# Pinning TensorE's issue order, splitting the load of p, and two w_out tiles with buffers of their own

## The chip, the core and the metric

The kernel runs on one core of a Trainium2 chip. The metric is the device time of one launch in microseconds (us). TensorE (PE) multiplies, VectorE (DVE), ScalarE (ACT) and GpSimd (POOL) work element by element, and SyncE (SP) issues nearly all DMAs. Each engine works through its own stream of instructions in the order in which they were issued to it, and waits on semaphores for the others.

## What is computed

```python
def sm_attn(qq, kk, vv):                      # softmax(qq kk^T / 8) vv
    ...
p_packed = sm_attn(p, k, v)                   # 32 rows per head
x = sm_attn(q, p_packed, p_packed)            # (4, 8, 576, 64) -> (2304, 512)
h = x @ w_in                                  # (2304, 2048)
x = (max(h, 0) + log1p(exp(-abs(h)))) @ w_out # (2304, 512)
out = (sigmoid(x @ w_gate) * (x @ w_val)) @ w_out2
```

q, k, v and p come in float32; the weights come in float64 and are turned into float32 on DVE from their two 32-bit words.

## The kernel before

**Attention** runs in 8 units (batch b, head group g of four heads). A unit is a generator of 11 stages (`attn_unit`, line 330): three stages of transposes of k (L333 is the transpose of p, L313 those of k and q), then the first scores (L326, with kT and pT) and their softmax on DVE and ACT (L345 to L357, up to the DVE transpose a1T), three stages of transposes of q, the product with v (L369), the second scores (L326, with qT and ppT), and the second softmax (L391 to L409), whose result is split into a high part A2h (ACT, L410) and a low part A2l (POOL, L101 with A2l). `att_tick` advances one live unit by one stage; up to four units run ahead before the first layer.

**The first layer** goes over entries (b, c), b a batch and c one of 8 chunks of 256 columns of w_in. The matrix p_packed is first multiplied into w_in (`prep_wp`, L480, then ACT writes the high part wph at L487, DVE or POOL the low part wpl at L101). `emit_h` then does 12 matmuls into one h tile (L113, L114, L115: the high and low products of A2 and wp), followed by softplus on ACT (L509 to L511) and DVE (L519, tile g). `emit_out1` multiplies the result ghl with w_out two entries later (L537, L538, L540) and DVE adds it into xa (L98 or L545). In the program's text `emit_h` of an entry stands ahead of the `emit_out1` of an older entry and ahead of the attention stages called between its pieces.

**The second layer** (L812 to L867, from about 400 us) is untouched but for two helpers through which its matmuls now go.

**What sets the order.** The text fixes one order in which instructions are traced. The framework then plans each engine's stream itself with a model of times: an instruction whose inputs it takes to be ready may be issued ahead of one that stands before it in the text. SP's stream is planned in the same way, and its DMAs wait there for the buffers that they write.

**Loads.** `load_kqv` (line 229) gives k, q, v tiles of 576 KB to ten places: eight in xa and NEXT = 2 tiles `own0`, `own1`; a tile is loaded when a place comes free. `load_next` (line 144) loads the next weight tile from the list `order` (two tiles of w_in chunk 0, two of w_out chunk 0, two of w_in chunk 1, and so on) into one of two `raw` buffers; `convert` (L189, L194, L198 on DVE) frees it and calls `load_next` again. p, 0.5 MB, is loaded by two DMAs on ACT's queue (L275) into `pall`, for all 8 units at once.

Of the kernel before, what the change touches and what calls it, by code (L numbers as in the profile page):

```python
# [11 lines left out]
I32 = mybir.dt.int32  # L12
# [8 lines left out]
def attn_moe_moe_kernel(  # L21
# [24 lines left out]
    nc = tc.nc  # L46
    B, H, S, D = q.shape
    NK = p.shape[2]
    NT, DM = out.shape
    F1 = w_in.shape[1]  # L50
    F2 = w_gate.shape[1]
    P = 128
# [6 lines left out]
    KD = DM // P  # L59
# [8 lines left out]
    L0 = 3  # L68
    GP = 7
    PO = ['k0', 'q0', 'k1', 'v0', 'q1', 'v1']  # L70
    XR = 0
    EARLY = [0]
    NCV = 5
    SC = float(D) ** -0.5
# [11 lines left out]
    xa = cst.tile([P, KD * NT], F32, name="xa")  # L86
# [16 lines left out]
    def pool_hi(hi, x):  # L103
        nc.gpsimd.tensor_scalar(hi, x, 1.0, 0.0, op0=ALU.mult, op1=ALU.add)

    def hi_of(on_act, hi, x):
        if on_act:
            nc.scalar.activation(hi, x, AF.Copy)  # L108
        else:
            pool_hi(hi, x)  # L110

    def mm3(ps, wh, wl, xh, xl, first, last):
        nc.tensor.matmul(ps, wh, xh, start=first, stop=False)  # L113
        nc.tensor.matmul(ps, wh, xl, start=False, stop=False)  # L114
        nc.tensor.matmul(ps, wl, xh, start=False, stop=last)  # L115

    nc.scalar.preload_act_table_set("natural_log_exp_and_others")

    att = tc.alloc_tile_pool(name="att", bufs=1, side="right")
# [14 lines left out]
    for c in range(NCH1):  # L134
        order += [("in", c, f) for f in range(2)] + [("out", c, f) for f in range(2)]
        if c > ECS:
            n = -(-len(early) // (NCH1 - c))
# [6 lines left out]
    def load_next():  # L144
        if not waiting:
            return
        nm, c, f = key = waiting.popleft()
        if XR and key == ("out", 0, 0):

            t = xa[:, : 2 * DM].bitcast(I32).rearrange("p (n t) -> p n t", t=2)  # L150
        else:
            t = raw.tile([P, KD * P, 2], I32, tag="raw", name="raw_" + nm)
        a = c * CF + f * P
        if nm in ("out", "o2"):
            nc.sync.dma_start(t.rearrange("p n t -> p (n t)"), w32[nm][a : a + P, :])
        elif nm == "in":

            for g in range(2):
                nc.sync.dma_start(
                    t[64 * g : 64 * g + 64].rearrange("p (k n) t -> p k (n t)", k=KD),  # L160
                    w32[nm][256 * g : 256 * g + 256, 2 * a : 2 * (a + P)].rearrange(
                        "(k p) x -> p k x", p=64
                    ),
                )
        else:
            nc.sync.dma_start(
                t.rearrange("p (k n) t -> p k (n t)", k=KD),
                w32[nm][:, 2 * a : 2 * (a + P)].rearrange("(k p) x -> p k x", p=P),
            )
        raws[key] = t  # L170
# [41 lines left out]


    KQV = 2 * NC * D
    NEXT = 2
    own = [att.tile([P, KQV], F32, name=f"own{i}") for i in range(NEXT)]
    plan = deque((nm, u) for u in range(2 * B) for nm in "kqv")
    first = sorted((plan.popleft() for _ in range(6)), key=lambda x: PO.index(x[0] + str(x[1])))
# [3 lines left out]
    def place(u):  # L222

        for tag in [*range(2 * (u // 2), 2 * B), *range(2 * B, 2 * B + NEXT)]:
            if tag not in busy:
# [37 lines left out]
    ident = cst.tile([P, P], F32, name="ident")  # L263
# [7 lines left out]


    pall = att.tile([P, 2 * B, 2, D], F32, name="pall")
    for i in range(2):
        nc.scalar.dma_start(  # L275
            pall[:, :, i], p.rearrange("b (g h) n d -> (h n) (b g) d", g=2)
        )

    NWORK = 7
    SPL = []  # L280
# [27 lines left out]
    def turned(src, dst):  # L308

        for i in range(0, NC, 3):  # L310
            ps = bank1()
            for c in range(i, i + 3):
                nc.tensor.transpose(  # L313
                    ps[:, (c - i) * P : (c - i + 1) * P], src[:, c * P : (c + 1) * P], ident
                )
            o = dst[:, i : i + 3].rearrange("p c n -> p (c n)")
            nc.scalar.activation(o, ps[:, : 3 * P], AF.Copy)
            yield

    def scores(lhsT, xT, to):  # L320

        for e in range(2):
            r = slice(64 * e, 64 * e + 64)
            for h in range(4):
                n = slice(NK * h, NK * h + NK)
                nc.tensor.matmul(  # L326
                    to[e][n], lhsT(r, h), xT[r, :, n], start=True, stop=True
                )

    def attn_unit(u):  # L330
        b, g = divmod(u, 2)
        px = bank1()
        nc.tensor.transpose(px[:, :P], pall[:, u].rearrange("p i d -> p (i d)"), ident)  # L333
        pT = att.tile([P, P], F32, tag="pT", bufs=2, name="pT")
        nc.scalar.activation(pT, px[:, :P], AF.Copy)
        kT = att.tile([P, NC, P], F32, tag="kT", bufs=1, name="kT")
# [28 lines left out]
        for e in range(2):  # L365
            for c in range(NC):
                for h in range(4):
                    r = slice(NR * h, NR * h + NR)
                    nc.tensor.matmul(  # L369
                        pp[h // 2][64 * (h % 2) : 64 * (h % 2) + 64, :NK],  # L370
                        vt[r, c, e, :], a1T[r, e * NC + c, :],
                        start=e == c == 0, stop=(e, c) == (1, NC - 1),
                    )
# [75 lines left out]
    w_in_f, wo_hl, Wp = {}, {}, {}  # L449
# [18 lines left out]
    def prep_wp(items):  # L468

        n = len(items)  # L470
        hi, lo = (
            ph1.tile([P, 2, 2, CF], F32R, tag="wp" + y, bufs=NWP, name="wp" + y)[:, :n]
            for y in "hl"
        )
        ps = [bank1().rearrange("p (i n) -> p i n", i=2)[:, :n] for _ in range(2)]
        for i, (b, c) in enumerate(items):
            for h in range(4):
                for t in range(2):
                    r = slice(64 * t, 64 * t + 64)
                    nc.tensor.matmul(  # L480
                        ps[t][NK * h : NK * h + NK, i], ppT[r, b, 4 * t + h, :],
                        w_in_f[c][r, h, :], start=True, stop=True,
                    )
            Wp[b, c] = (hi[:, i], lo[:, i])
        for t in range(2):
            if n == 1 or items[0][0] == items[1][0]:
                nc.scalar.activation(hi[:, :, t], ps[t], AF.Copy)  # L487
                split_lo(nc.vector, lo[:, :, t], ps[t], hi[:, :, t])
            else:
                x = new_cv().rearrange("p (i n) -> p i n", i=2)  # L490
                nc.scalar.activation(x, ps[t], AF.Copy)
                pool_hi(hi[:, :, t], x)
                split_lo(nc.gpsimd, lo[:, :, t], x, hi[:, :, t])
            yield
# [33 lines left out]
    def emit_out1(b, c, s, att_ticks):  # L528
        finish(f"wo{c}")
        gh, gl = gt.pop((b, c, s))  # L530
        for m in range(KD):
            ms = slice(m * P, (m + 1) * P)
            ps = bank1()
            out_ = ps[:, :HS]
            for f in range(2):
                wh, wl = wo_hl[c, f]
                nc.tensor.matmul(out_, wh[:, ms], gh[:, f], start=f == 0, stop=False)  # L537
                nc.tensor.matmul(out_, wl[:, ms], gh[:, f], start=False, stop=False)  # L538
            for f in range(2):
                nc.tensor.matmul(out_, wo_hl[c, f][0][:, ms], gl[:, f], start=False, stop=f == 1)  # L540
            dst = x2(b, s)[:, m]
            if c == 0:
                copy(CP0, dst, out_)
            else:
                nc.vector.tensor_tensor(dst, dst, out_, op=ALU.add)  # L545
            between(m, att_ticks)
# [147 lines left out]
    load_kqv(6)  # L694
    for _ in range(2):
        load_next()
    units.extend(range(2 * B))
    n = 0
    jobs.append(("win0", prep_win(0)))
# [18 lines left out]
    for i, (b, c) in enumerate(entries):  # L718
# [9 lines left out]
        if c >= 2 and b % 2 == 0:  # L728
# [3 lines left out]
            if k + 1 < len(groups):  # L732
                x, cc = groups[k + 1]
# [33 lines left out]
            pend.append((b, c, s))  # L767


    if PRE:  # L770
        tc.keep_in_program_order(nc.scalar.preload_act_table_set("sigmoid_and_others"))
    while pend:
        emit_out1(*pend.popleft(), [0] * 3)
# [79 lines left out]
    def emit_out2(ps, c, t):  # L853
        bank = bank1()
        ts_ = slice(t * P, (t + 1) * P)
        for f in range(2):
            gh, gl = (y.rearrange("p b s t -> p (b s t)") for y in gv[ps, 2 * c + f])
            _, _, oh, ol = Bop[ps, 2 * c + f]
            nc.tensor.matmul(bank, gh[:, ts_], oh, start=f == 0, stop=False)  # L859
            nc.tensor.matmul(bank, gh[:, ts_], ol, start=False, stop=False)  # L860
            nc.tensor.matmul(bank, gl[:, ts_], oh, start=False, stop=f == 1)  # L861
        i = KD * HS * HB * 2 * ps + DM * t
        acc = xa[:, i : i + DM]
        if c == 0:
            copy(CPA, acc, bank)
        else:
            nc.vector.tensor_tensor(acc, acc, bank, op=ALU.add)  # L867
        tick()
        if c == NCH2 - 1:
            t0 = ps * HB * S + t * P  # L870
            a, e = t0, t0 + P
            while a < e:
                b, r = divmod(a, S)
                ee, cc = divmod(r // NR, NC)
                nc.sync.dma_start(outv[b, ee, cc], acc[a - t0 : a - t0 + NR])
                a += NR
# [63 lines left out]
```

## Time and profile before

| | us |
|---|---|
| median of 3 runs | 885.74 (882.08 to 887.05) |
| the profiled execution | 884.71 |
| its span | 882.9 |
| outside the span | 1.8 |
| PE busy | 823.5 (93%) |
| DVE, POOL, ACT busy | 626.0, 451.9, 376.3 |

PE is the busiest engine by far, so its idle time and the stretches in which its clock was granted at half are what can be won back. A row of the timeline has start, duration, engine, line, operation, tiles and count, and in brackets the engine's idle time before it with what ended it.

### The profile page before, as it was taken

The numbers are of one execution on the slowest core, as the hardware profiler recorded it, in microseconds if no ns is written. First come the engines' busy times: TensorE is split into PE (matmuls) and PEld (weight loads), VectorE is DVE, ScalarE is ACT, GpSimd is POOL, SyncE is SP. The second block draws the span as 40 slices with busy tenths as digits, with TensorE's granted clock in tenths as the row PEclk, the third lists the DMA queues.
The fourth block names the chain that finished last, engine by engine and source line by source line (L and its number), as shares of the span: only waits on it lengthen the run. The fifth ranks groups of instructions, "written<-read, shape, count | busy, mean of one in ns | idle before, by whom it ended". The sixth has DMA issues, their size and how long they took to land.

```text
span 882.9 us, 17370 instructions
## 1 busy us (share of the span) xinstructions
PE 823.5 (93%) x7040; PEld 755.4 (86%) x7040; DVE 626.0 (71%) x1057; ACT 376.3 (43%) x659; POOL 451.9 (51%) x420
## 2 busy tenths in 40 slices
PE   2976999999999999998999999999989999999995
PEld 1655788889989999998989999999869999999984
DVE  0757676778686577558898688897898656766763
ACT  1453666466555556666633331232342432322210
POOL 0043232366473555576469687886883633634400
PEclk9787999999999999998999999999999999999998
DMA  8644030123152223100055454645435312213004
GB/s 266 220 139 122 28 110 29 31 67 97 39 172 60 49 70 110 43 25 1 1 170 177 155 168 150 186 129 157 139 87 141 86 48 71 79 44 95 13 1 107
DMA packets 52480, 85.67 MB, mean 97 GB/s; under 512 B 6960, under 2 KB 30640, under 8 KB 52400
## 3 DMA queue, kind: packets, MB, share of 16 engines
q1 hardware_dynamic: 50320, 84.04, 32.5%
q8 instruction: 55, 0.90, 0.4%
q10 hardware_dynamic: 2080, 0.52, 0.3%
q14 instruction: 25, 0.20, 0.1%
HBM read 65.67 MB, written 18.87 MB: 96 GB/s over the span
## 4 chain that ended last, share of the span: by engine, by line
PE 77%; DVE 11%; ACT 3%; DMA 3%; issue 3%; POOL 2%; SPq 0%; POOLq 0%; ACTq 0%; DVEq 0%
PE bank L115 9%; PE bank L113 9%; PE bank L114 9%; PE ps L537 6%; PE ps L540 6%; PE ps L538 6%; PE ps L861 5%; PE ps L859 5%; PE ps L860 5%; PE ps L115 3%; PE ps L114 3%; PE ps L113 3%; DMA pall<-in_p_dram 2%; PE ps L369 2%; PE ps L313 2%
## 5 line engine op out<-in xcount | busy, mean ns | idle before, releaser
L113 PE MATMUL bank<-aop,BH 128*128 128x288 f32 x672 | 198.8, 296 | 3.7 <-DVE work L824 1.5
L114 PE MATMUL bank<-aop,BH 128*128 128x288 f32 x672 | 197.9, 295 | 1.0 <-DVE aop L101 0.9
L115 PE MATMUL bank<-aop,BL 128*128 128x288 f32 x672 | 198.6, 296 | 0.0
L101 POOL TENSOR_TENSOR ghl<-g,ghl 128x576 fp32r<-128x576 f32 x64 | 93.8, 1469 | 133.5 <-ACT ghl L108 133.5
L537 PE MATMUL ps<-ghl,woh 128*128 128x288 f32 x512 | 148.7, 305 | 6.0 <-DVE xa L545 3.6
L538 PE MATMUL ps<-ghl,wol 128*128 128x288 f32 x512 | 144.6, 297 | 0.0
L545 DVE TENSOR_TENSOR xa<-xa,ps 128x288 f32<-128x288 f32 x224 | 97.2, 448 | 59.0 <-PE ps L540 58.0
L113 PEld LDWEIGHTS bank<-aop,BH 128*128 128x128 f32 x672 | 126.2, 188 | 9.1 <-issue 1.4
L114 PEld LDWEIGHTS bank<-aop,BH 128*128 128x128 f32 x672 | 126.4, 188 | 5.1 <-DVE aop L101 1.6
L115 PEld LDWEIGHTS bank<-aop,BL 128*128 128x128 f32 x672 | 126.5, 188 | 0.0
L101 POOL TENSOR_TENSOR BL<-cv,BH 128x512 fp32r<-128x512 f32 (+1 forms) x96 | 116.8, 1231 | 11.3 <-ACT BH L108 10.2
L537 PEld LDWEIGHTS ps<-ghl,woh 128*128 128x128 f32 x512 | 97.4, 190 | 15.9 <-DVE xa L545 6.2
L540 PE MATMUL ps<-ghl,woh 128*128 128x288 f32 x512 | 110.6, 297 | 0.1
L538 PEld LDWEIGHTS ps<-ghl,wol 128*128 128x128 f32 x512 | 97.5, 190 | 0.5 <-issue 0.5
L812 DVE TENSOR_TENSOR work<-work,bank 128x576 f32<-128x576 f32 (+1 forms) x100 | 70.8, 725 | 29.8 <-PE bank L115 29.4
L859 PE MATMUL ps<-oh,gv 128*128 128x512 f32 x216 | 84.6, 392 | 1.3 <-DVE xa L867 0.8
L860 PE MATMUL ps<-ol,gv 128*128 128x512 f32 x216 | 84.8, 393 | 0.0
L861 PE MATMUL ps<-oh,gv 128*128 128x512 f32 x216 | 84.7, 393 | 0.0
L113 PE MATMUL ps<-A2h,wph 128*128 128x288 f32 x256 | 78.6, 309 | 6.3 <-ACT A2h L410 2.7
L540 PEld LDWEIGHTS ps<-ghl,woh 128*128 128x128 f32 x512 | 83.1, 189 | 0.4 <-POOL ghl L101 0.4
L867 DVE TENSOR_TENSOR xa<-xa,ps 128x512 f32<-128x512 f32 x90 | 61.5, 684 | 27.4 <-PE ps L861 26.9
L114 PE MATMUL ps<-A2l,wph 128*128 128x288 f32 x256 | 77.7, 304 | 1.9 <-POOL A2l L101 1.9
(115 smaller groups left out, 1576.0 us busy)
## 6 DMA issues: line engine op xcount, KB each, us to landing
cv<-B SPq DMA_DIRECT2D x52, 256.0 KB, 2.7
B<-cv SPq DMA_DIRECT2D x48, 256.0 KB, 4.2
raw_in<-in_moe_w_in_dram SPq DMA_DIRECT2D x32, 256.0 KB, 4.1
raw_out<-in_moe_w_out_dram SPq DMA_DIRECT2D x16, 512.0 KB, 3.7
raw_g<-in_moe_w_gate_dram SPq DMA_DIRECT2D x12, 512.0 KB, 4.0
raw_v<-in_moe_w_val_dram SPq DMA_DIRECT2D x12, 512.0 KB, 4.4
raw_o<-in_moe_w_out_dram SPq DMA_DIRECT2D x12, 512.0 KB, 4.2
out_dram<-xa SPq DMA_DIRECT2D x72, 64.0 KB, 1.7
```

The source lines that it names most:

```text
L101: eng.tensor_tensor(lo, x, hi.bitcast(F32), op=ALU.subtract)
L113: nc.tensor.matmul(ps, wh, xh, start=first, stop=False)
L114: nc.tensor.matmul(ps, wh, xl, start=False, stop=False)
L115: nc.tensor.matmul(ps, wl, xh, start=False, stop=last)
L537: nc.tensor.matmul(out_, wh[:, ms], gh[:, f], start=f == 0, stop=False)
L538: nc.tensor.matmul(out_, wl[:, ms], gh[:, f], start=False, stop=False)
L540: nc.tensor.matmul(out_, wo_hl[c, f][0][:, ms], gl[:, f], start=False, stop=f == 1)
L545: nc.vector.tensor_tensor(dst, dst, out_, op=ALU.add)
L812: nc.vector.tensor_tensor(to, x, y, op=ALU.add)
L859: nc.tensor.matmul(bank, gh[:, ts_], oh, start=f == 0, stop=False)
L860: nc.tensor.matmul(bank, gh[:, ts_], ol, start=False, stop=False)
L861: nc.tensor.matmul(bank, gl[:, ts_], oh, start=False, stop=f == 1)
```

## The change

A wrapper `matmul` (and `transpose`) pins each PE instruction behind the one traced before it, until `strict[0]` is set to False after the first layer's loop. p is loaded for unit 0, then for unit 1, by four small DMAs on ACT's queue; the other six units' p goes to SP's queue behind the first six k, q, v tiles and the first two w_in tiles. The first two w_out tiles get buffers of their own, so that four weight tiles are asked for at the start instead of two; NEXT falls from 2 to 1 to make room.

```diff
-    XR = 0
+    FIRST = [("out", 0, 0), ("out", 0, 1)]
...
+    strict = [True]
+
+    def matmul(*args, **kw):
+
+        i = nc.tensor.matmul(*args, **kw)
+        return tc.keep_in_program_order(i) if strict[0] else i
+
+    def transpose(to, x):
+        i = nc.tensor.transpose(to, x, ident)
+        return tc.keep_in_program_order(i) if strict[0] else i
+
     def mm3(ps, wh, wl, xh, xl, first, last):
-        nc.tensor.matmul(ps, wh, xh, start=first, stop=False)
...
+        matmul(ps, wh, xh, start=first, stop=False)
...
-        if XR and key == ("out", 0, 0):
-
-            t = xa[:, : 2 * DM].bitcast(I32).rearrange("p (n t) -> p n t", t=2)
+        if key in FIRST:
+            t = att.tile([P, KD * P, 2], I32, name=f"raw_first{c}{f}")
         else:
             t = raw.tile([P, KD * P, 2], I32, tag="raw", name="raw_" + nm)
...
-    NEXT = 2
+    NEXT = 1
...
-    for i in range(2):
-        nc.scalar.dma_start(
-            pall[:, :, i], p.rearrange("b (g h) n d -> (h n) (b g) d", g=2)
-        )
+
+    def load_p(eng, a, e):
+        src = p.rearrange("b (g h) n d -> (h n) (b g) d", g=2)
+        for i in range(2):
+            eng.dma_start(pall[:, a:e, i], src[:, a:e])
+
+    load_p(nc.scalar, 0, 1)
+    load_p(nc.scalar, 1, 2)
...
     load_kqv(6)
+    for _ in range(2):
+        load_next()
+    load_p(nc.sync, 2, 2 * B)
     for _ in range(2):
         load_next()
     units.extend(range(2 * B))
...
+    strict[0] = False
     if PRE:
```

In the same way the other calls of `nc.tensor.matmul` and `nc.tensor.transpose` become `matmul` and `transpose`.

## Rows read from the trace of the kernel before

**Rows 1.** Engine table by stretch: busy us (count) per engine, PEclk, DMA share, GB/s.
```profile
0.00:17.40 17.40, 0.00 (x0) 0.03 (x1) 0.00 (x0) 1.28 (x1) 0.70 (x6) 1.00 0.92 278
...
68.00:74.00 6.00, 0.23 (x8) 0.23 (x16) 5.88 (x13) 1.08 (x2) 0.00 (x0) 0.75 0.26 81
74.00:82.00 8.00, 7.06 (x43) 5.81 (x28) 6.20 (x11) 2.30 (x5) 2.43 (x2) 0.55 0.48 136
...
200.00:400.00 200.00, 197.23 (x1715) 189.64 (x1713) 137.48 (x267) 121.45 (x192) 116.36 (x101) 1.00 0.26 73
```
**Rows 2.** PE's waits over the span, longest first: us in total, times, longest.
```profile
PE ps L333 <- DMA pall<-in_p_dram: 17.4, 1, 17.4
PE ps L480 <- DVE w_in L198: 5.9, 1, 5.9
```
**Rows 3.** Landing time of p's two DMAs, and of k of unit 1, issued at 1.66.
```profile
DMA to landing us min/median/max: 6.0/11.0/16.0
...
DMA to landing us min/median/max: 7.9/7.9/7.9
```
**Rows 4.** Timeline of PE, 17 to 39 us: unit 0's transposes and scores; unit 2's p.
```profile
20.55 1.21 PE L326 MATMUL ps<-kT,pT 64*32 64x288 f32 x16
...
38.64 0.47 PE L333 MATMUL ps<-ident,pall 128*128 128x128 f32 x1
```
**Rows 5.** Timeline of SP, 4 to 34 us.
```profile
4.89 13.00 SPq L159 DMA_DIRECT2D raw_in<-in_moe_w_in_dram  x4
...
28.69 4.03 SPq L155 DMA_DIRECT2D raw_out<-in_moe_w_out_dram  x2
```
**Rows 6.** DMA queues from 0 to 18 us (q10 is p).
```profile
q10 hardware_dynamic: 2080, 0.52, 14.0%
```
**Rows 7.** Timeline of DVE, 61 to 74 us.
```profile
61.57 0.76 DVE L519 SCALAR_TENSOR_TENSOR g<-ps,t 128x576 f32<-128x576 f32 x1 [7.23 <-ACT t L511]
...
63.53 1.64 DVE L189 TENSOR_SCALAR w_in<-raw_in 128x512 int32<-128x512 int32 x1
```
**Rows 8.** Timeline of PE, 43 to 61 us: the first h tile, b = 0.
```profile
44.59 0.40 PE L113 MATMUL ps<-A2h,wph 128*128 128x288 f32 x1 [0.32 <-ACT wph L487]
...
56.07 0.61 PE L114 MATMUL ps<-A2l,wph 128*128 128x288 f32 x1 [0.97 <-POOL A2l L101]
```
**Rows 9.** PE by line, 44.5 to 56.0 us.
```profile
L326 PE MATMUL ps<-kT,pT 64*32 64x288 f32 x16 | 2.0, 415 | 0.0
...
L313 PE MATMUL ps<-ident,xa 128*128 128x128 f32 x9 | 1.5, 273 | 0.0
```
**Rows 10.** Timeline of PE, 97 to 101 us: first h tile of b = 1.
```profile
97.27 0.40 PE L537 MATMUL ps<-ghl,woh 128*128 128x288 f32 x1 [0.67 <-ACT pT L335]
...
100.70 0.40 PE L115 MATMUL ps<-A2h,wpl 128*128 128x288 f32 x1 [0.40 <-DVE wpl L101]
```
**Rows 11.** PE by line, 74.7 to 78.1 us (chunk 1), then 133.9 to 136.1 us (b = 2).
```profile
L537 PE MATMUL ps<-ghl,woh 128*128 128x288 f32 x2 | 1.0, 524 | 0.0
...
L537 PE MATMUL ps<-ghl,woh 128*128 128x288 f32 x4 | 1.2, 324 | 0.0
```
**Rows 12.** Timeline, 128 to 134 us: SP's load of unit 7's q; PE, unit 7 and b = 2.
```profile
129.06 0.33 SPq L236 DMA_DIRECT2D own<-in_q_dram  x1
...
130.89 0.49 PE L313 MATMUL ps<-ident,own 128*128 128x128 f32 x3
```
**Rows 13.** The landing time of that load.
```profile
DMA to landing us min/median/max: 3.8/3.8/3.8
```
**Rows 14.** Timeline of PE, 164 to 174 us: first h tile of b = 3.
```profile
166.88 0.40 PE L113 MATMUL ps<-A2h,wph 128*128 128x288 f32 x1 [0.89 <-ACT wph L487]
...
173.38 0.40 PE L114 MATMUL ps<-A2l,wph 128*128 128x288 f32 x1 [0.69 <-POOL A2l L101]
...
178.16 0.37 PE L113 MATMUL ps<-A2h,wph 128*128 128x288 f32 x1 [0.81 <-DVE g L519]
```
**Rows 15.** PE by line, 164.75 to 173.35 us.
```profile
L537 PE MATMUL ps<-ghl,woh 128*128 128x288 f32 x12 | 3.5, 302 | 0.0
```

More of the change, by code (lines that the diff above doesn't have):

```diff
@@ L110, in hi_of @@
             pool_hi(hi, x)
+    strict = [True]
[5 more added lines that the diff above has]
+        return tc.keep_in_program_order(i) if strict[0] else i
     def mm3(ps, wh, wl, xh, xl, first, last):
-        nc.tensor.matmul(ps, wh, xh, start=first, stop=False)
-        nc.tensor.matmul(ps, wh, xl, start=False, stop=False)
-        nc.tensor.matmul(ps, wl, xh, start=False, stop=last)
+        matmul(ps, wh, xh, start=first, stop=False)
+        matmul(ps, wh, xl, start=False, stop=False)
+        matmul(ps, wl, xh, start=False, stop=last)
     nc.scalar.preload_act_table_set("natural_log_exp_and_others")
@@ L312, in turned @@
             for c in range(i, i + 3):
-                nc.tensor.transpose(
-                    ps[:, (c - i) * P : (c - i + 1) * P], src[:, c * P : (c + 1) * P], ident
-                )
+                transpose(ps[:, (c - i) * P : (c - i + 1) * P], src[:, c * P : (c + 1) * P])
             o = dst[:, i : i + 3].rearrange("p c n -> p (c n)")
@@ L325, in scores @@
                 n = slice(NK * h, NK * h + NK)
-                nc.tensor.matmul(
+                matmul(
                     to[e][n], lhsT(r, h), xT[r, :, n], start=True, stop=True
@@ L332, in attn_unit @@
         px = bank1()
-        nc.tensor.transpose(px[:, :P], pall[:, u].rearrange("p i d -> p (i d)"), ident)
+        transpose(px[:, :P], pall[:, u].rearrange("p i d -> p (i d)"))
         pT = att.tile([P, P], F32, tag="pT", bufs=2, name="pT")
@@ L368, in attn_unit @@
                     r = slice(NR * h, NR * h + NR)
-                    nc.tensor.matmul(
+                    matmul(
                         pp[h // 2][64 * (h % 2) : 64 * (h % 2) + 64, :NK],
@@ L479, in prep_wp @@
                     r = slice(64 * t, 64 * t + 64)
-                    nc.tensor.matmul(
+                    matmul(
                         ps[t][NK * h : NK * h + NK, i], ppT[r, b, 4 * t + h, :],
@@ L536, in emit_out1 @@
                 wh, wl = wo_hl[c, f]
-                nc.tensor.matmul(out_, wh[:, ms], gh[:, f], start=f == 0, stop=False)
-                nc.tensor.matmul(out_, wl[:, ms], gh[:, f], start=False, stop=False)
+                matmul(out_, wh[:, ms], gh[:, f], start=f == 0, stop=False)
+                matmul(out_, wl[:, ms], gh[:, f], start=False, stop=False)
             for f in range(2):
-                nc.tensor.matmul(out_, wo_hl[c, f][0][:, ms], gl[:, f], start=False, stop=f == 1)
+                matmul(out_, wo_hl[c, f][0][:, ms], gl[:, f], start=False, stop=f == 1)
             dst = x2(b, s)[:, m]
@@ L858, in emit_out2 @@
             _, _, oh, ol = Bop[ps, 2 * c + f]
-            nc.tensor.matmul(bank, gh[:, ts_], oh, start=f == 0, stop=False)
-            nc.tensor.matmul(bank, gh[:, ts_], ol, start=False, stop=False)
-            nc.tensor.matmul(bank, gl[:, ts_], oh, start=False, stop=f == 1)
+            matmul(bank, gh[:, ts_], oh, start=f == 0, stop=False)
+            matmul(bank, gh[:, ts_], ol, start=False, stop=False)
+            matmul(bank, gl[:, ts_], oh, start=False, stop=f == 1)
         i = KD * HS * HB * 2 * ps + DM * t
```

## The prediction

> **What bounds the kernel now.** I read the engine table first: PE is busy for 823.5 of 882.9 us, and no other engine comes near. So the time is PE's work plus the holes in it, and I then asked by stretch where the holes are. From 200 us on there is nothing that this change touches: 197.23 of 200 us busy from 200 to 400 [rows 1]. The holes that it can touch lie in the first 200 us. PE does nothing for the first 17.4 us [rows 1]. The list of PE's waits names the cause: one wait of 17.4 us for p [rows 2]. The reader should see in it that only p was late: k of unit 1, third in the queue, landed at 1.66 + 7.9 = 9.6 us, while p's second DMA needed 16.0 us [rows 3]. The second longest wait is L480's, 5.9 us, for the conversion of w_in chunk 1 on DVE [rows 2]; the stretch from 68 to 74 us has 0.23 us of PE work, and the next 8 us run at a mean granted clock of 0.55, that is mostly at the lower of the two levels, 1.2 GHz [rows 1].
>
> **Price of a matmul.** In the dense stretch from 200 to 400 us, 1715 matmuls take 197.23 us, 0.115 us each [rows 1]. I use that for work that is moved.
>
> **p first and alone.** The first PE work needs p of unit 0 and k of unit 0. With the text's order kept, the first scores (20.55 us now, [rows 4]) also stand behind the first transposes of unit 1, so behind k of unit 1. p's traffic took 14.0% of the DMA engines over 18 us, 2.5 us of all of them [rows 6]; some 1 us of that lay ahead of k of unit 1, so I let it land near 8.6 us, and the scores start near 9.1. That is 11.4 us earlier. The bounds: 10.5 if k of unit 1 lands no earlier than now, 12.4 if unit 0 alone decided. What covers the rest of p: it goes behind the first w_in tiles and is needed by unit 2, whose first row comes at 38.64, 18 us after the first scores [rows 4]; if that cover fails, it is the third rival. p also stops holding up SP: the four w_in issues took 13.00 us, the last one going out only when p had landed [rows 5]. Term: **-11.4**.
>
> **Two w_out tiles with own buffers.** Now the first w_out issue waits until 28.69 us for a raw buffer [rows 5], and k, q, v of later units stand behind it on SP. With own buffers that wait goes, and w_in chunk 1 can be loaded as soon as chunk 0 is converted. The end of that conversion is what the issue at 28.69 waited for, 35 us before the conversion of chunk 1 starts at 63.53, behind the g tiles (L519) for which DVE waited 7.23 us [rows 7]. That the data are there much earlier lets the plan put the conversion into DVE's idle time; I take it so, and the 5.9 us wait goes. What is late next there is the chain from L480 to wpl, which is counted below. The clock: 7.06 us of work from 74 to 82 ran at 0.55 [rows 1] and would take about 3.9 at full clock; without the 6 us hole in front I take 2.5 of these 3.2 back. Terms: **-5.9 and -2.5**, bounds 0 and -9.1 together. Two buffers take the room of one own tile. One place fewer means that a few loads go out one event later. The tight one is unit 7's k: it would get the slot in SP's stream that unit 7's q has now, 129.06 us [rows 12], and land 3.8 us later [rows 13], at 132.9, while PE wants it at 130.89 [rows 12]. Term: **+2.0**, bounds 0 (another place is free) and +4 (a raw tile's wait ahead of it on SP).
>
> **The text's order on PE.** Nothing is added to PE; what changes is what may run while a matmul waits. Wherever the plan let something overtake, the wait is now bare, and all that stands behind it on PE waits too. I looked at every first h tile of a batch, since it stands behind a fresh A2 and a fresh wp.
> Batch 0: its first matmul ran at 44.59, but A2l of unit 1 was ready only for 56.07 [rows 8]. In between PE did 16 score matmuls and 18 transposes (two groups of 9, one of them shown) of units 2 and 3 [rows 9]: some 4.7 us of PE time that now comes after the wait. DVE and POOL, without these units' softmax in between, should bring A2l about 1 to 2 us sooner. Term **+3.5**, bounds 0 and +4.7.
> Batch 0, second chunk: 6 matmuls of out1 (2 of them L537, [rows 11]) overtook the wait for wph and wpl: **+0.7**. Batch 1: from 97.27 to 100.70 two pieces of out1, 12 matmuls [rows 10], **+1.4**, and the clock may fall there, up to +2.5. Batch 2, the same pattern with 4 rows of L537, so 9 to 12 matmuls [rows 11]: **+1.1**; bounds for these three from 0 (the wait shrinks) to double.
> Batch 3: the first h matmul ran at 166.88, and A2l of unit 7 came for 173.38 [rows 14]; out1 filled the time from 164.75 on, its 12 matmuls of L537 standing for 36 with L538 and L540 [rows 15], 36 x 0.115 = 4.2 us, of which a later wait of 0.81 us [rows 14] takes in a part: **+3.4**, bounds +2 and +5. This leaves PE with a handful of matmuls in some 8.6 us; a hole of that kind (68 to 74 us) was followed by a low clock [rows 1], which I price like that one: **+2.5**, bounds 0 and +3.2.
> After batch 3 the plan mostly put h tiles ahead of out1; inputs of both were there long before, so the order costs nothing, bounds -2 and +2.
> Here the trace shows a waiting PE row with nothing behind it slipping past: 5.9 us idle ahead of L480 [rows 2]. The Trainium skill states the same as a rule ("TensorE: Matmul & The Clock Gate", Part 3, on what overlaps and what doesn't): weight loads may be pulled ahead, matmuls start and end in strict program order. By that rule a pinned wait costs all the matmuls that used to overtake it, which is the first rival; the trace agrees as far as the one wait goes.
>
> **Sum**, against the profiled execution (884.7; the median of the runs is 1.0 higher): -11.4 - 5.9 - 2.5 + 2.0 + 3.5 + 0.7 + 1.4 + 1.1 + 3.4 + 2.5 = -5.2, so **879.5**. Gains of 19.8 stand against costs of 14.6: the sign hangs on two or three terms.
>
> **Rivals.**
> 1. *Slower: the bare waits win.* Place: the first h tile of each batch. If the conversion of w_in chunk 1 stays behind the g tiles, the 8.4 go, and the sum is -11.4 + 14.6 = +3.2; with batch 0 at its upper bound (+1.2) and a low clock at batch 1 too (+2.0 of the 2.5) it is +6.4: **891**. It decides from the point where bare waits cost over 11.4 us in all. For: DVE takes its stream in order, and L519 stood ahead of L189 [rows 7]. Against: the data now come far earlier, and DVE had 7.23 us idle there.
> 2. *Much faster: the waits shrink.* With PE held, DVE, ACT and POOL have less to do between the links of a waiting chain, so that A2l and wpl come sooner. Half of the 12.6 us of order terms would go: 879.5 - 6.3 = **873**. For: from 68 to 74 us DVE is busy for 5.88 of 6 us while PE waits [rows 1]. Against: that the chain of unit 7 is mostly its own links.
> 3. *The head start is given back.* The rest of p and two w_out tiles, 1.4 MB, stand ahead of unit 2's k and q on SP; if unit 2 comes late for PE by the whole head start: 879.5 + 11.4 = **891**. Against: at 278 GB/s, the mean of the first 17.4 us [rows 1], 1.4 MB is 5 us, and unit 2 has more slack than that.
> 4. *The pin does nothing*, as the new plan would have kept the text's order anyway, at these places too, without longer waits: -19.8, **865**. Against: all four batches overtook.
>
> **How the numbers follow.** Chances: forecast 0.43, rival 1 0.20, rival 2 0.25, rival 3 0.07, rival 4 0.05. The forecast's own range is 874 to 885. The range 867 to 892 takes in rivals 1, 2 and 3 and leaves out most of rival 4 and the tails. About 0.5% (4.4 us) is what a measurement of this kernel can tell from no change. Faster by more than that: rival 2, rival 4 and just under half of the forecast, 0.50; slower: three quarters of rival 1, half of rival 3 and a tail, 0.20; the rest, 0.30, is within it.
>
> **What would show it.** The first PE row near 5 us and the first scores near 9; w_out's first issue before 20 us; no wait of L480 for the w_in conversion; waits of L113 and L114 for A2h and A2l of 5 us or more at the first h tile of batches 0 and 3, with no L537 between L480 and L113 there; a wait of 2 us at unit 7's k. If the waits of PE at these tiles come to less than 6 us in all, the order cost less than I say; if L480 still waits for DVE, the slower rival is right. A second layer (from 400 us) that takes longer or shorter by over 3 us would make the whole sum wrong, as I hold it still.

## The result, and the profile after

| | before | after |
|---|---|---|
| median of 7 runs, us | 885.0 | 892.6 |
| ratio | | 1.0089 (1.0067 to 1.0112) |
| profiled execution, its span, us | 884.7, 882.9 | 894.3, 892.5 |
| PE busy, us | 823.5 | 828.5 |

The change makes the kernel 0.9% slower, about 7.9 us, where 879.5 was forecast. (One of the seven runs after took 1598 us and is left out of the ratio.) In the kernel after, the wrappers stand for all lines of PE: every matmul is a row of L116 and every transpose one of L120, so rows are told apart by their tiles. The add of out1 into xa is L557 there (L545 before), wph is L499, g is L531.

PE's table by stretch, after (busy us, count, granted clock, DMA share, GB/s), to be read beside [rows 1]:
```profile
0.00:20.00 20.00, 11.63 (x210) 1.00 0.98 294
20.00:50.00 30.00, 18.94 (x236) 0.56 0.74 239
50.00:80.00 30.00, 26.99 (x458) 0.82 0.34 96
80.00:100.00 20.00, 16.42 (x152) 0.83 0.17 49
100.00:160.00 60.00, 55.56 (x1022) 1.00 0.17 55
160.00:180.00 20.00, 12.55 (x88) 0.74 0.17 53
...
200.00:400.00 200.00, 193.37 (x1655) 0.99 0.25 73
```
The start is won: PE works 11.63 us of the first 20. Then come 30 us at a mean clock of 0.56, a hole at 160 to 180 us, and, where [rows 1] has 197.23 us of work from 200 to 400 us, 193.37. The 1.00 of the first stretch is not borne out by the rows in it: the first sixteen scores, below, take 1.21 us, as sixteen do at a granted clock of 0.50 in the kernel with fillers further down, where sixteen at 1.00 take 0.72.

The first rows of PE, after, to be read beside [rows 4]:
```profile
6.61 0.45 PE L120 MATMUL ps<-ident,pall 128*128 128x128 f32 x1 [6.61 <-DMA pall<-in_p_dram]
...
10.33 0.45 PE L120 MATMUL ps<-ident,pall 128*128 128x128 f32 x1 [1.35 <-DMA pall<-in_p_dram]
...
11.35 1.21 PE L116 MATMUL ps<-kT,pT 64*32 64x288 f32 x16
```
PE's waits after (us in total, times, longest), to be read beside [rows 2]:
```profile
PE ps L116 <- ACT A2h L422: 10.6, 2, 6.9
PE ps L116 <- DVE xa L557: 9.3, 10, 1.9
PE ps L120 <- DMA pall<-in_p_dram: 8.0, 2, 6.6
PE ps L116 <- ACT wph L499: 6.1, 5, 2.3
```
The wait of L480 for the conversion of w_in, 5.9 us in [rows 2], is gone. In its place stand bare waits: for A2h, for wph, and ten times for the add of out1, where the kernel before had 3 such waits with 3.6 us in all.

**A table by places in the text.** Since both kernels have the same PE instructions, one can ask when each has done all PE work up to the same place of the program's text. The columns are one profiled execution each, as the difference to the kernel before in us (the experiments are named below):

| place | before at | after | no order | order only | p only | buffers only |
|---|---|---|---|---|---|---|
| unit 0's product with v | 28.9 | -8.8 | -9.3 | -1.0 | -9.5 | -1.3 |
| batch 0, second chunk | 79.5 | -11.8 | -9.6 | -7.0 | -5.9 | -8.0 |
| ahead of batch 1's first h tile | 95.5 | -11.0 | -11.2 | -3.8 | -1.5 | -9.6 |
| ahead of batch 1's fourth h tile | 119.2 | -7.2 | -11.4 | +0.2 | -1.8 | -9.9 |
| ahead of batch 3's first h tile | 164.8 | -4.4 | -10.5 | +1.2 | -2.1 | -8.8 |
| behind the first entry of chunk 2 | 199.1 | +2.2 | -10.5 | +8.8 | -2.0 | -8.8 |
| early in the second layer | 460.4 | +9.6 | -12.4 | +13.3 | -4.3 | -10.5 |
| end | 873.3 | +9.7 | -12.4 | +13.5 | -4.2 | -10.4 |

An end in this table can lie 3 us or so beside the medians, which decide. What it shows is where time goes: after is 11 us ahead at 95 us, and gives that back and more: at batch 1 (3.8), between there and batch 3 (2.8), at batch 3 (6.6) and, spread out, from 200 us on (7.4). From 460 us on nothing changes.

### The profile page after: what moved, and what is told of

Read it like the earlier page. It is cut to its first block, busy times and chain, and to the rows that moved or that the text cites. A ratio compares the mean times of both kernels' runs of the same rounds, so it can differ in the third digit from the quotient of the medians.

```text
span 892.5 us, 17375 instructions
## 1 busy us (share of the span) xinstructions
PE 828.5 (93%) x7040; PEld 757.4 (85%) x7040; DVE 629.9 (71%) x1057; ACT 379.7 (43%) x659; POOL 453.1 (51%) x420
## 4 chain that ended last, share of the span: by engine, by line
PE 73%; DVE 14%; DMA 4%; ACT 4%; issue 2%; POOL 1%; ACTq 0%; SPq 0%; DVEq 0%; POOLq 0%
PE ps L116 45%; PE bank L116 27%; DVE aop L101 2%; DMA raw_out<-in_moe_w_out_dram 2%; DVE xa L557 2%; DVE sum L604 1%; PE ps L120 1%; DMA raw_v<-in_moe_w_val_dram 1%; DMA pall<-in_p_dram 1%; ACT aop L597 1%; DVE g L531 1%; DVE ps L199 1%; DVE ps L204 1%; DVE xa L883 0%; DVE bank L828 0%
## 5 line engine op out<-in xcount | busy, mean ns | idle before, releaser
L116 PE MATMUL bank<-aop,BH 128*128 128x288 f32 x1344 | 271.2, 295 | 4.7 <-DVE work L840 1.7
L116 PE MATMUL ps<-ghl,woh 128*128 128x288 f32 x1024 | 228.9, 303 | 11.1 <-DVE xa L557 9.3
L116 PEld LDWEIGHTS bank<-aop,BH 128*128 128x128 f32 x1344 | 220.2, 188 | 14.2 <-DVE aop L101 1.6
L116 PE MATMUL bank<-aop,BL 128*128 128x288 f32 x672 | 198.6, 296 | 0.0
L116 PEld LDWEIGHTS ps<-ghl,woh 128*128 128x128 f32 x1024 | 173.6, 191 | 21.7 <-DVE xa L557 14.5
L116 PE MATMUL ps<-oh,gv 128*128 128x512 f32 x432 | 148.2, 392 | 1.3 <-DVE xa L883 0.8
L557 DVE TENSOR_TENSOR xa<-xa,ps 128x288 f32<-128x288 f32 x224 | 96.6, 448 | 72.1 <-PE ps L116 71.3
L116 PE MATMUL ps<-ghl,wol 128*128 128x288 f32 x512 | 145.4, 298 | 0.0
L116 PEld LDWEIGHTS bank<-aop,BL 128*128 128x128 f32 x672 | 126.5, 188 | 0.0
L101 POOL TENSOR_TENSOR BL<-cv,BH 128x512 fp32r<-128x512 f32 (+1 forms) x96 | 117.0, 1234 | 11.2 <-ACT BH L108 10.1
L116 PEld LDWEIGHTS ps<-ghl,wol 128*128 128x128 f32 x512 | 98.2, 192 | 0.0
L116 PEld LDWEIGHTS ps<-oh,gv 128*128 128x128 f32 x432 | 80.9, 188 | 16.9 <-DVE xa L883 2.0
L116 PE MATMUL ps<-A2h,wph 128*128 128x288 f32 x256 | 79.5, 310 | 16.7 <-ACT A2h L422 10.6
L116 PE MATMUL ps<-ol,gv 128*128 128x512 f32 x216 | 84.8, 393 | 0.0
L116 PE MATMUL ps<-A2h,wpl 128*128 128x288 f32 x256 | 79.1, 309 | 2.3 <-DVE wpl L101 2.3
L116 PE MATMUL ps<-A2l,wph 128*128 128x288 f32 x256 | 78.2, 306 | 2.5 <-POOL A2l L101 2.5
L857 ACT ACTIVATE work<-bank 128x576 f32<-128x576 f32 (+1 forms) x25 | 15.8, 634 | 145.0 <-DVE bank L828 145.0
L828 DVE TENSOR_TENSOR bank<-work,bank 128x576 f32<-128x576 f32 (+1 forms) x75 | 54.8, 736 | 32.1 <-PE bank L116 31.8
L521 ACT ACTIVATE t<-ps 128x576 f32<-128x576 f32 x64 | 41.6, 649 | 65.0 <-PE ps L116 64.8
```

What stands on the lines that cost most here:

```text
L101: eng.tensor_tensor(lo, x, hi.bitcast(F32), op=ALU.subtract)
L116: i = nc.tensor.matmul(*args, **kw)
L521: nc.scalar.activation(t1, h, AF.Abs)
L828: nc.vector.tensor_tensor(to, x, y, op=ALU.add)
L857: nc.scalar.activation(s1, g1, AF.Sigmoid)
```

## The experiments

The edits are given against the changed kernel unless another is named. Ratios are to the kernel before, run on the same chip; in us they are taken of 885.0.

**No order on PE.** `strict = [False]`, so that p first and the two own buffers are left.

> The changed kernel without the order on TensorE: p of the first units first and the two w_out tiles with own buffers remain. Theory (the order is what costs): the first PE row stays near 6.6 us and the first scores near 11.3, no wait of the matmul on w_in for its conversion, and the 9 to 11 us by which the changed kernel was ahead at 90 us last to the end: 874 us (872 to 877). Rival (the head start is lost anyway, through later k, q, v loads and through DVE): 883 to 889, with new PE waits for k, q or v of units 4 to 7.

Ratio 0.9899 (0.9873 to 0.9925), and 0.9896 (0.9876 to 0.9916) in a second measurement further down: 9 us faster than before. The theory holds: the order costs, the loads gain. But the gain is only half of the 17.8 us that the forecast had for p and the buffers.

**Order only.** The kernel before's loads, with the wrappers.
```diff
-    FIRST = [("out", 0, 0), ("out", 0, 1)]
+    FIRST = []
-    NEXT = 1
+    NEXT = 2
-    load_p(nc.scalar, 0, 1)
-    load_p(nc.scalar, 1, 2)
+    load_p(nc.scalar, 0, 2 * B)
...
-    for _ in range(2):
-        load_next()
-    load_p(nc.sync, 2, 2 * B)
```


> The kernel before with nothing but the order on TensorE. Theory (the costs of the order are separate from the loads and add up): some 11 us up to 180 us and some 7.5 us from 200 to 400 us, 903 us (898 to 908). Rival (the bare waits were long only because the earlier start moved them to a busier DVE): 892 or less, with fewer than 6 us of waits at the first h tiles of batches 0 and 3.

Ratio 1.0133 (1.0095 to 1.0172), 11.8 us, between the two values named; the rival's second sign is not there, as the two waits for A2h at these tiles come to 8.3 us. The costs don't simply add: on the new loads the same order costs 1.0089 - 0.9899, 16.8 us. The table shows why: with the old loads the order gains 3.8 us by 95 us, since it too removes the wait of L480 (no row of it is left). With the own buffers that gain had been made already.

**Where the order costs: ended at chunk 2, begun at chunk 2, ended ahead of batch 3.** Three kernels, each with a line in the loop over entries; the second starts with `strict = [False]`.
```diff
+        if (b, c) == entries[8]:       # 1st: ended at chunk 2
+            strict[0] = False
...
+        if (b, c) == entries[8]:       # 2nd: begun at chunk 2
+            strict[0] = True
...
+        if (b, c) == (3, 0):           # 3rd: ended ahead of batch 3
+            strict[0] = False
```


> The changed kernel, with the order on TensorE ended where the first h tile of chunk 2 stands in the text (near 190 us). Theory (from 200 us on each pass of out1 opens with a bare wait for DVE's add that frees its PSUM bank, where the plan used to put an h tile ahead): those waits (6.5 us between 200 and 360) go, 885 us (883 to 888). Rival (that loss is left over from the state before 200 us: loads or DVE behind their time): no change, 891 to 894.

> The changed kernel, with the order on TensorE only from the first h tile of chunk 2 to the end of the first layer. Theory: as without any order (874) plus the same 7 us: 881 us (879 to 884), with 5 to 7 us of PE waits for the add of out1 between 200 and 400 us. Rival (a loss left over from earlier): 874, with less than 3 us of these waits.

> The changed kernel, with the order on TensorE ended ahead of batch 3 (near 155 us). Theory (the bare wait of batch 3's first h tile and the low clock after it cost 6 us by themselves, as the step of the forecast had it): 879 us (877 to 881), against some 884 with the order up to 190 us, and no stretch of low clock from 160 to 180 us. Rival (out1 is used up by then in any order, so that batch 3 waits all the same): 884 us, with the granted clock of 160 to 180 us under 0.9.

Ratios 0.9998 (0.9979 to 1.0018), 0.9991 (0.9958 to 1.0023) and 0.9959 (0.9936 to 0.9983). So the order costs 0.9959 - 0.9899 = 5.3 us up to batch 3, 0.9998 - 0.9959 = 3.5 us at batch 3, and from chunk 2 on 8.1 us, both as 1.0089 - 0.9998 and as 0.9991 - 0.9899. The theory of each holds, but for the price in the third: of the 6 us for batch 3, 3.5 came out. (Each of these differences carries some 3 us either way, from the intervals of its two ratios.) PE's waits from about 190 to 400 us, first of the kernel with the order ended at chunk 2, then with the order begun there, and PE's stretch from 160 to 180 us with the order ended ahead of batch 3:
```profile
PE ps L116 <- DVE xa L557: 1.6, 1, 1.6
```
```profile
PE ps L116 <- DVE xa L557: 6.4, 8, 1.5
```
```profile
160.00:180.00 20.00, 17.20 (x167) 1.00 0.18 53
```
With the order ended there that stretch has 17.20 us of work at full clock, with it 12.55 at 0.74 (above).

**What the late waits are.** Two rows of PE in the kernel after, and DVE's beside them:
```profile
255.02 0.43 PE L116 MATMUL ps<-ghl,woh 128*128 128x288 f32 x2
257.38 0.40 PE L116 MATMUL ps<-ghl,woh 128*128 128x288 f32 x1 [1.93 <-DVE xa L557]
```
```profile
255.55 0.69 DVE L199 TENSOR_SCALAR ps<-raw_v 128x512 int32<-128x512 int32 x1 [1.42 <-DMA raw_v<-in_moe_w_val_dram]
256.27 0.69 DVE L204 SCALAR_TENSOR_TENSOR ps<-raw_v,ps 128x512 int32<-128x512 int32 x1
256.88 0.81 DVE L557 TENSOR_TENSOR xa<-xa,ps 128x288 f32<-128x288 f32 x2
```
PE has filled three banks with pieces of out1 and needs a fourth. The add that would free one stands in DVE's stream behind two steps of a weight's conversion, and those behind a load. All six gaps of over 0.6 us from 200 to 400 us are at such a fourth piece. Where the order was free, h tiles with inputs long ready ran among the pieces. In the kernel before, at the same six places, the plan had put ten matmuls of the next h tile ahead of the second piece at five of them, fourteen more ahead of the fourth as well at two, and at the longest gap a whole h tile ahead of the first. The first of the six in the kernel before, with pieces beginning at 206.49, 208.60 and 212.04 (the third is left out):
```profile
206.49 0.29 PE L537 MATMUL ps<-ghl,woh 128*128 128x288 f32 x1
...
207.28 0.29 PE L113 MATMUL ps<-A2h,wph 128*128 128x288 f32 x1
...
208.60 0.29 PE L537 MATMUL ps<-ghl,woh 128*128 128x288 f32 x1
...
210.18 0.29 PE L114 MATMUL ps<-A2l,wph 128*128 128x288 f32 x1
...
212.04 0.29 PE L537 MATMUL ps<-ghl,woh 128*128 128x288 f32 x1
```
Two runs asked whether the bank or DVE's stream is the cause.

*The fourth piece later.* For chunk 2 and later, the fourth piece of out1 stands in the text behind the next h tile.
```diff
-            ps = bank1()
...
+            if hold and m == KD - 1:
+                held.append(piece)
+            else:
+                piece()
...
             emit_h(b, c, s)
+            flush()
```


> The changed kernel, order on TensorE and all; only the fourth piece of each out1 of chunk 2 and later stands in the text behind the next h tile, as the plan placed it where the order was free. Theory (each of the ten bare waits for the add of out1 is at the fourth piece, whose PSUM bank comes free last; 12 matmuls of an h tile in front cover 1.6 us): the waits of 200 to 400 us fall from 6.5 to under 2 us and the time to 886 us (885 to 888). Rival (the wait moves with the bank ring to another piece): 890 to 893 us, with the same sum of waits.

Ratio 1.0107 (1.0079 to 1.0136): no gain over 1.0089. The waits of 195 to 400 us did fall, to
```profile
PE ps L116 <- DVE xa L564: 3.8, 7, 1.6
```
with the longest now at the third piece behind an h tile. The theory had under 2 us and 886; the waits fell by less and the time not at all, which is nearer to the rival. The rows of the kernel before, above, say where the theory was wrong: the plan had not put the h tile ahead of the fourth piece throughout, but chose anew at each place, and one fixed move is not the same. A part of the gain may be there all the same: from the first entry of chunk 2 to early in the second layer this execution lost 4.9 us on the kernel before, where the kernel after lost 7.4. But it was 1.9 us further behind at chunk 2 already, and the medians can't tell so little.

*Conversions not in PSUM.* `CPS = 0`: from chunk 2 on, too, a conversion works in place in SBUF and takes no bank of the ring, except those of w_val, which still write a bank. Its first two steps are also no longer handed out together.

> The changed kernel, order and all; the conversions of weights work in place in SBUF, not through a PSUM bank of the ring that the out1 pieces use. Theory (out1's bare waits of 200 to 400 us come from that ring of four banks: conversions take banks and hold them for three DVE operations): these waits fall from 6.5 to under 2.5 us, a ratio to the kernel before of 1.001 to 1.004. Rival (what is waited for is DVE's place in its stream, the add standing behind conversions whatever bank they use): waits of 5 us or more remain, ratio 1.007 to 1.011.

Ratio 1.0367 (1.0345 to 1.0389), and 8.0 us of these waits: the theory fell, but the run doesn't single out the bank, for the conversion itself became slower. By line (busy us, mean ns), after, then this kernel:
```profile
L204 DVE SCALAR_TENSOR_TENSOR ps<-raw_out,ps 128x512 int32<-128x512 int32 x10 | 7.0, 696 | 0.3
```
```profile
L204 DVE SCALAR_TENSOR_TENSOR cv<-raw_out,cv 128x512 int32<-128x512 int32 x14 | 20.2, 1450 | 0.0
```
Four of the 14, ahead of chunk 2, work in SBUF in both kernels. What slows these steps can be read in this kernel's trace, from three of DVE and the rows of POOL beside them (POOL's next begins at 297.12):
```profile
290.35 1.42 DVE L204 SCALAR_TENSOR_TENSOR cv<-raw_out,cv 128x512 int32<-128x512 int32 x1
...
292.42 1.18 DVE L208 SCALAR_TENSOR_TENSOR cv<-raw_out,cv 128x512 int32<-128x512 int32 x1
293.52 0.68 DVE L204 SCALAR_TENSOR_TENSOR cv<-raw_out,cv 128x512 int32<-128x512 int32 x1
```
```profile
288.44 2.78 POOL L101 TENSOR_TENSOR wpl<-cv,wph 128x512 fp32r<-128x512 f32 x2
291.18 1.87 POOL L101 TENSOR_TENSOR ghl<-g,ghl 128x576 fp32r<-128x576 f32 x1
```
The first two steps each end 0.55 us after an instruction of POOL has ended (at 291.22 and 293.05); the third, with POOL idle, takes 0.68 us, as a step through PSUM does. The Trainium skill ("SBUF — State Buffer", Terms) says that DVE and GpSimd share one pair of SBUF ports, which one holds for a whole instruction while the other waits. The trace agrees with it here. So the run made DVE slower and can't tell how much of the waits is the ring of banks: that they follow DVE's stream is likely, and the rest stays open.

**p only, and buffers only,** both without the order. p only: `FIRST = []`, `NEXT = 2`, and the last two `load_next` dropped. Buffers only: `load_p(nc.scalar, 0, 2 * B)` in place of the three calls.

> The kernel before, with p of units 0 and 1 first and the rest of p behind the first w_in tiles, nothing else; no order on TensorE. Theory (the head start of 9 us melts to some 2 to 4 us before the matmuls on w_in, since PE falls into the low clock earlier, and the wait for the conversion of w_in chunk 1 stays): 881 to 883 us, with a wait of 4 us or more at these matmuls. Rival (the head start lasts to the end): 876 us.

> The kernel before, with the two own buffers of w_out (and one place fewer for k, q, v), nothing else; p as before, no order on TensorE. Theory (the 5.9 us wait for the conversion of w_in goes and the clock after it is full): 877 to 879 us, no wait at the matmuls on w_in of chunk 1. Rival (the conversion stays behind the g tiles on DVE): 884 to 886 us with that wait in place.

Ratios 0.9956 (0.9934 to 0.9979) and 0.9932 (0.9903 to 0.9961): 3.9 us and 6.0 us, together 9.9, beside 9 for both at once. p only has this among its waits, while buffers only has no row of it:
```profile
PE ps L116 <- DVE w_in L208: 6.4, 1, 6.4
```
The theory of each holds. With p alone most of the head start is gone from DVE's stream by 45 us: w_in's chunk 1 goes into the raw buffers that DVE's conversion of w_out frees. SP's four issues of it, in the kernel before, then with p alone:
```profile
44.10 9.56 SPq L159 DMA_DIRECT2D raw_in<-in_moe_w_in_dram  x4
```
```profile
45.70 6.06 SPq L169 DMA_DIRECT2D raw_in<-in_moe_w_in_dram  x4
```
The first goes out later than in the kernel before, the last (51.76 against 53.66) 1.9 us earlier, where PE had been 9.5 us ahead. (These loads land some 7 us before their conversion begins, so they are a sign of it and not the wait itself.)

**One own buffer, two places for k, q, v,** without the order: `NEXT = 2`, `FIRST` of one tile, one `load_next` less.

> As the kernel without the order (both load changes), but with one own buffer for w_out in place of two and two own places for k, q, v in place of one. Theory (one place fewer costs 2 us through unit 7's k, as the step of the forecast had it): 2 us faster than the kernel without the order, a ratio to the kernel before of 0.987 to 0.989. Rival (the place is not missed; the second buffer is what lets w_in chunk 1 come early): slower than the kernel without the order, ratio 0.992 to 0.996.

Ratio 0.9972 (0.9952 to 0.9992): slower, as the rival had it, and past its range too. The wait for w_in comes back with 3.6 us, so it takes both buffers to remove it; what the place costs this run can't tell.

**What takes the head start of p: extra traffic.** In the kernel before, six copies of unit 0's first softmax to a scratch tensor. The question came from a row of the kernel without the order, a hole with no releaser:
```profile
23.46 0.64 PE L116 MATMUL ps<-qT,ppT 64*32 64x288 f32 x1 [2.50 <-issue]
```


> The kernel before with 1.8 MB of idle traffic added (six copies of unit 0's first softmax to a scratch tensor, from 26 us on), at the time when a 16 KB packet of instructions is fetched (27 to 28 us). Theory (the hole of 2.1 to 2.5 us that the trace of the kernels with p first shows at the tenth matmul of q of unit 0, with no releaser, is TensorE waiting for its next instructions behind loads): a hole of 1.5 us or more appears at that same matmul (near 30 us), where the kernel before has none. Rival (the hole has to do with the kernels' other waits): no hole there, PE dense from 29 to 31 us.

At the following matmul a hole came, but a small one:
```profile
29.51 0.33 PE L313 MATMUL ps<-ident,xa 128*128 128x128 f32 x1 [0.35 <-issue]
```
The one run took 884.0 us. The theory asked for 1.5 us or more at the same matmul, so this run doesn't bear it out; what the 2.50 us are stays open.

**What takes the head start of p: fillers,** without the order.
```diff
     make_identity(nc, ident)
+    warm = bank1()
+    for _ in range(24):
+        tc.keep_in_program_order(
+            nc.tensor.matmul(warm[:, :P], ident, ident, start=True, stop=True)
+        )
```


> The kernel without the order (both load changes), with 24 idle matmuls of the identity with itself at the head of TensorE's stream, where it waits for p until 6.6 us; they read nothing else and are done before p lands. Theory (the head start from p first is taken back by the low clock, which in all kernels so far began 16 to 17 us after TensorE's first work, whatever followed): the clock falls near 18 us in place of 23, and the kernel is 1 to 3 us slower than the one without the fillers. Rival (the clock follows the holes of the attention chain near 21 us): it falls at 23 us as before, with no difference over 1 us. Third (a busier start keeps the clock up): it falls later than 25 us, and the kernel is faster by 2 us or more.

> The kernel without the order once more, beside the one with the fillers and with more rounds, as the fastest version so far: 0.990 of the kernel before (0.987 to 0.9925), if p first and the two own buffers are worth some 9 us together.

Ratios 0.9889 (0.9863 to 0.9914) with the fillers, 0.9896 (0.9876 to 0.9916) without. The first theory got the clock right and the time wrong. With the fillers, PE's stretches from 18 us, and its first and second scores, the second of which the plan now put behind a wait (they were at 15.95 without the fillers):
```profile
18.00:24.00 6.00, 3.02 (x84) 0.55 1.03 388
24.00:40.00 16.00, 16.00 (x274) 0.50 0.83 246
```
```profile
11.02 0.72 PE L116 MATMUL ps<-kT,pT 64*32 64x288 f32 x16
...
19.33 1.21 PE L116 MATMUL ps<-kT,pT 64*32 64x288 f32 x16 [5.56 <-ACT kT L334]
```
The low clock began 3.6 and 6.5 us earlier than in the two executions without fillers, PE was through with unit 0's product with v 7 us later (2.2 us ahead of the kernel before in place of 9.3), and yet by the second chunk of batch 0 it was 9.5 us ahead, as the kernel without fillers is, and the end is the same. So what PE reaches in the first 30 us hardly decides the end; and the low clock of that stretch doesn't either. Buffers only says the same: 8.0 us behind the kernel without the order at unit 0's product, 2.0 behind it at the end. The theory's "16 to 17 us" is not one distance for all kernels: from TensorE's first row to the fall of the clock it is 13.9 us in order only, 18.0 with one own buffer and 17.3 with the fillers.

## Why the prediction was wrong

Forecast sum: -5.2 us. Measured: +7.9. By parts, each as the difference of two ratios:

| part | forecast | measured |
|---|---|---|
| p first | -11.4 | -3.9 |
| own buffers, with unit 7's k | -6.4 | -6.0 |
| both together | -17.8 | -9.0 |
| order up to batch 3 | +6.7 | +5.3 |
| order at batch 3 | +5.9 | +3.5 |
| order after batch 3 | 0 (-2 to +2) | +8.1 |

Each measured part carries some 3 us either way.

**Two steps failed**, by about 8 us each.

*"After batch 3 the plan mostly put h tiles ahead of out1; inputs of both were there long before, so the order costs nothing."* Inputs were ready, but an instruction also needs a place for its result, and I did not ask for that. out1's fourth piece waits for the add that frees its bank, and the h tiles that the plan put among the pieces were the cover. I had the row for it in hand, the third in the list of the kernel before that [rows 2] is taken from:
```profile
PE ps L537 <- DVE xa L545: 3.6, 3, 2.1
```
And the dense 197.23 us of [rows 1] were read as "nothing that this change touches" when they were the plan's work. Priced right, this step alone turns the sign, 879.5 + 8.1 = 887.6, and so does the next, with 8.8 us less for both loads: 888.3.

*"That is 11.4 us earlier."* The first scores came at 11.35, 9.2 us earlier than in [rows 4], and the reason is a load that I left out. k of unit 1 landed at 1.66 + 6.2 = 7.9, before the 8.6 that I gave it; but p of unit 1 is transposed ahead of the first scores too, and PE waited for it until 10.33. That is a miss of 2 us. The larger one is that the whole head start was carried to the end. PE has holes and half-clock stretches until 100 us (0.56, 0.82 and 0.83 in its table above), and in them a later start is caught up and an earlier one lost. With p alone, where the wait for w_in stays, 9.5 us of lead are 1.5 by 95 us, and with the fillers a lead of 2.2 turns into the same 11 as one of 9.3. The third rival (the head start is given back, 0.07) was right that it is lost, which the larger part is, and wrong on the cause: in the kernel after, the one row of PE waiting for a load after p is 1.0 us for a k. With p alone SP's rows above show most of it gone from DVE's stream by 45 us; which link sets the time at 70 to 95 us I haven't shown.

**What held.** The buffers: L480's wait is gone and the gain is the forecast's within the interval (-3.5 to -8.6). Unit 7's k: forecast +2.0, and PE waits 1.0 us for it:
```profile
126.05 0.85 PE L120 MATMUL ps<-ident,xa 128*128 128x128 f32 x6 [1.01 <-DMA xa<-in_k_dram]
```
The order at batch 3, 5.9 forecast, is 6.6 in the table and 3.5 by the medians. PE's rows there, to be read beside [rows 14], have A2h and A2l as named, and matmuls of 0.44 us behind them:
```profile
168.17 0.61 PE L116 MATMUL ps<-A2h,wph 128*128 128x288 f32 x1 [3.75 <-ACT A2h L422]
169.64 0.61 PE L116 MATMUL ps<-A2l,wph 128*128 128x288 f32 x1 [0.87 <-POOL A2l L101]
170.05 0.44 PE L116 MATMUL ps<-A2h,wpl 128*128 128x288 f32 x1
```
The order up to batch 3 came out near its sum, but by two errors. At batch 0, forecast +3.5 and +0.7, the bare wait is there and costs nothing that lasts, as at 95 us the kernel with the order and the one without are level (-11.0, -11.2). At batch 1, forecast +1.4, it is 3.8 us. The rows of batch 0, then of batch 1, beside [rows 8] and [rows 10]:
```profile
44.99 0.61 PE L116 MATMUL ps<-A2h,wph 128*128 128x288 f32 x1 [6.87 <-ACT A2h L422]
46.83 0.61 PE L116 MATMUL ps<-A2l,wph 128*128 128x288 f32 x1 [1.23 <-POOL A2l L101]
```
```profile
87.82 0.40 PE L116 MATMUL ps<-A2h,wph 128*128 128x288 f32 x1 [2.27 <-ACT wph L499]
89.67 0.61 PE L116 MATMUL ps<-A2h,wpl 128*128 128x288 f32 x1 [1.31 <-DVE wpl L101]
```
I had priced batch 1 by the 12 matmuls that overtook (1.4 us). The bare waits are 3.6 us, longer than the work that used to fill them, and the second is followed by matmuls at half clock. The first rival had the sign, with 891, but its place only in part: it looked for the bare waits at the first h tiles alone, and half of them are in the dense first layer; and L480's wait, on which its sum was built, is gone. The fourth rival's sum left out unit 7's k: with its +2.0 it is -17.8, so 867.

**A version that beats both** is the one without the order: p first and both own buffers, 0.99 of the kernel before.

## What to carry to other kernels

A dense stretch under a planned order is dense because of the plan; before fixing its order, ask of each instruction that was moved not only when its inputs are ready but which buffer it writes and who frees that. Price a wait laid bare by the length of the wait, not by the work that used to hide it. A head start counts only where the engine is busy from there on: on an engine that waits for others again soon, take what is left of it behind the last such wait.

## What was unexpected of the hardware

The granted clock fell in the middle of work and stayed low through work without a gap. In the kernel with buffers only:
```profile
24.00:34.00 10.00, 9.00 (x270) 1.00 0.46 140
34.00:40.00 6.00, 6.00 (x110) 0.50 0.96 342
```
and with the fillers it was 0.50 through 16.00 us of unbroken work (above). And a conversion step with both inputs in SBUF took 1.45 us in the mean, against 0.70 with its intermediate result in PSUM, because it waited for POOL: beside an idle POOL it took 0.68.
